# Attention's main loop ordered by timed events, the product with v in two lumps a pair

## The chip, the cores and the metric

One core of a Trainium2 chip runs the whole program. The metric is the device time of one execution in microseconds, the median of the runs of one kernel. Five engines matter here: TensorE (PE in the rows, its weight loads PEld), VectorE (DVE), ScalarE (ACT), GpSimd (POOL), and SyncE (SP), which here only issues DMAs. Each works through its own queue in order.

## The reference

What is computed is attention with rotary positions over 4 batches of 8 heads (576 positions, 64 wide), and two feed-forward layers on its output.

```python
def _attn_ref(q, k, v):                 # 4, 8, 576, 64
    ...
    q_rot, k_rot = (rotate(q), rotate(k))
    scores = scale * np.matmul(q_rot, k_rot.transpose(0, 1, 3, 2))
    scores = scores - np.max(scores, axis=-1, keepdims=True)
    attn = np.exp(scores)
    attn = attn / (np.sum(attn, axis=-1, keepdims=True) + 1e-09)
    return np.matmul(attn, v).astype(np.float32)

def reference(**kwargs):
    ...
    x = np.ascontiguousarray(attn_out.transpose(0, 2, 1, 3)).reshape(B * S, H * D)
    x = _moe_ref(x=x, **moe_kwargs)     # (max(x @ w_in, 0) ** 2) @ w_out, 2304 x 512, 2048 wide
    return _moe2_ref(x=x, **moe2_kwargs)  # leaky relu with alpha between two products
```

## The kernel before

Attention runs first, the two feed-forward layers (`moe`) after it. The change touches attention alone.

Attention works on 16 pairs of heads, one after another. The two heads of a pair (index j) lie side by side in the tiles. A pair has nine steps, (i, j) for four blocks i of 128 queries and both heads, and one step (4, 0) for the last 64 queries of both heads together.

In each step `scores` multiplies a block of q with all keys: k is split into a high and a low part (kH, kL), so a block is four matmuls, and ten in step (4, 0). They fill one of two score buffers `sc` (two PSUM banks each). VectorE takes the row maximum (L201), ScalarE the exp (L202), which writes the probabilities to `p` and their sum to `sums`. The next block for that buffer waits for the exp. Four steps later (LAG) `trans` turns the probabilities with four transpositions (L223) into a bank of the pool `ps_t`, and `leave` copies the bank to `pt`, on ScalarE and VectorE by turns. `trans_tail` (L235, L241, L242) does that for the 64 columns that are left over. `over` adds 1e-9 to the sums, takes their reciprocal (VectorE), transposes them (L254), and ScalarE copies and stores them to `rd`. `pv` multiplies the turned probabilities with v (L273), in two halves of 288 queries (hf 0 and 1), ten matmuls each; one matmul appears in the trace as two records. A half is copied to `st`, by VectorE for hf 0 (L278), by ScalarE for hf 1 (L280), and then stored to `xd` (L281).

The next pair's q and k come from `rope` on GpSimd. `turn` transposes them (L145, L151), each into a bank of `ps_t`; ScalarE copies the bank to the high part of `nat` (L139) and VectorE subtracts it from the bank for the low part (L140). `stack` then copies `nat` to kH, qT and kL with 12 DMAs of 144 KB on SP (L166). There is one `nat`.

PSUM has eight banks: four for the two score buffers, three for `ps_t` (NTB), one for the product with v (`ps_a`, NAC).

The order on TensorE and SP is the order in which the Python code issues (a manual schedule). ScalarE and VectorE follow a planner that goes by its own costs and that also chooses which free bank a tile gets. The loop goes over steps s: it issues the scores of step s, the transpositions of step s - 4, and then whatever `at_step` has put at s. The turning of the next pair stands at the pair's steps 0, 1 and 2 (the last with the tail and the stack). The sums follow straight after the tail of step (4, 0). The product with v stands in six lumps (LUMPS), of 4, 4 and 2 matmuls for each half, one behind each of the six steps after it; in the last pair each half is one lump. During the last 24 steps `follow` starts the loads and the first weight conversions of `moe`.

Of the kernel before, what the change touches and what calls it, by code (L numbers as in the profile page):

```python
# [22 lines left out]
P = 128  # L23
# [5 lines left out]
NQ = 5  # L29
NR = 10  # L30
SCALE = D ** -0.5

LAG = 4
# [6 lines left out]
OP0, OPD0, OP1, OPD1 = 1, 1, 0, 1  # L40
OP, OPD = 1, 1


def attention(tc, q, k, v, ident_d, rope_d, xd, rd, follow):
# [10 lines left out]
    with ExitStack() as at:  # L55
# [17 lines left out]
        ps_t = pool("ps_t", NTB, space=PSUM)  # L73
        ps_a = pool("ps_a", NAC, space=PSUM)

# [8 lines left out]

        pairs = [(b, hp) for b in range(B) for hp in range(NPAIR)]
        rot = {}
# [44 lines left out]

        def turn(n):


            nt = nat.tile([P, 2, 2, S + 64], F32R, name="nat")
            r4 = {nm: rot[n, nm].rearrange("p r j d -> p r (j d)") for nm in "kq"}

            def split(pv, view):
                A.activation(out=view(0), in_=pv, func=AF.Copy)  # L139
                V.tensor_tensor(out=view(1), in0=pv, in1=view(0).bitcast(F32), op=ALU.subtract)  # L140

            def main(x, nm):
                u = ps_t.tile([P, 512], F32, name="ps", tag="t")
                for c in range(4):
                    T.transpose(u[:, c * P:(c + 1) * P], r4[nm][:, c], ident)  # L145
                split(u, lambda y: nt[:, y, x, 64:576])

            def tail():
                u = ps_t.tile([P, 512], F32, name="ps", tag="t")
                for x, nm in enumerate("kq"):  # L150
                    T.transpose(u[:, x * P:(x + 1) * P], r4[nm][:, 4], ident)  # L151
                split(u[:, 0:256].rearrange("p (x z c) -> p x z c", x=2, z=2),
                      lambda y: nt[:, y].rearrange("p x (z c) -> p x z c", c=64)[:, :, 0:10:9])

            def stack():
                qT = qTs[n % 2]
                kH = kq.tile([P, 2 * S], F32R, name="kH")
                kL = kq.tile([P, 2 * S], F32R, name="kL")
                ops[n] = qT, kH, kL
                f = nt.bitcast(F32)  # L160
                for j in range(2):
                    for o, y, x, gap in ((kH, (0, 0), 0, 0), (qT, (0, 1), 1, 64), (kL, (1, 1), 0, 0)):
                        c0, o0 = 64 * (1 - j), j * (S + gap)
                        for z in range(2):
                            E = nc.scalar if z and n == 0 else nc.sync
                            E.dma_start(out=o[64 * z:64 * z + 64, o0:o0 + S].bitcast(F32),  # L166
                                        in_=f[64 * j:64 * j + 64, y[z], x, c0:c0 + S])

            def last():
                tail()  # L170
                stack()

            return [(main, 0, "k"), (main, 1, "q"), (last,)]

# [29 lines left out]

        turns = itertools.cycle((A, V))

        def leave(dst, src):
            E = next(turns)
            if E is A:
                A.activation(out=dst, in_=src, func=AF.Copy)  # L210
            else:
                V.tensor_copy(out=dst, in_=src)  # L212

        def trans(n, i, j):

            if (i, j) == (0, 0):
                PT[n, "tail"] = pt.tile([P, S], F32, name="ptt")
            if i == 0:
                PT[n, j] = pt.tile([P, 4, S], F32, name=f"pt{j}")
            p = Pt[n, i]  # L220
            u = ps_t.tile([P, 512], F32, name="ps", tag="t")
            for c in range(4):
                T.transpose(u[:, c * P:(c + 1) * P], p[:, (S + 64) * j + c * P:(S + 64) * j + (c + 1) * P], ident)  # L223
            uv = u.rearrange("p (c x) -> p c x", c=4)
            if i < 4:
                leave(PT[n, j][:, :, i * P:(i + 1) * P], uv)
            else:
                for x in range(2):
                    leave(PT[n, x][:, :, 512:576], uv[:, :, 64 * x:64 * x + 64])

        def trans_tail(n, i0, i1):

            u = ps_t.tile([P, 512], F32, name="ps", tag="t")
            for i in range(i0, min(i1, 4)):
                T.transpose(u[:, (i - i0) * P:(i - i0 + 1) * P], Pt[n, i][:, 512:640], ident)  # L235
            m = min(i1, 4) - i0
            if m:
                leave(PT[n, "tail"][:, i0 * P:(i0 + m) * P], u[:, 0:m * P])
            if i1 == 5:

                T.transpose(u[0:64, m * P:(m + 1) * P], Pt[n, 4][:, 512:576], ident)  # L241
                T.transpose(u[:, (m + 1) * P:(m + 2) * P], Pt[n, 4][:, 448:576], ident)  # L242
                for x in range(2):
                    rs, u0 = slice(64 * x, 64 * x + 64), (m + x) * P + 64 * x
                    leave(PT[n, "tail"][rs, 512:576], u[rs, u0:u0 + 64])

# [13 lines left out]

        accs = {}

        def pv(n, hf, c0, c1):
            b, hp = pairs[n]
            v2 = raw[n // 2 % 2, "v"][:, 2 * (n % 2):2 * (n % 2) + 2]
            sl = slice(hf * SH, (hf + 1) * SH)
            if c0 == 0:
                accs[hf] = ps_t.tile([P, 512], F32, name="ps", tag="t") if (n, hf) == (len(pairs) - 1, 1) else ps_a.tile([P, 512], F32, name="acc")
            acc = accs[hf]
# [14 lines left out]
        order = [(i, j) for i in range(4) for j in range(2)] + [(4, 0)]  # L284
        steps = [(n, i, j) for n in range(len(pairs)) for i, j in order]
        per = len(order)
        load(0, "k", 0, 1, nc.gpsimd)
# [11 lines left out]
        rope(0, "q", 5, NR, V)  # L299
        for f, *a in turn(0):  # L300
            f(*a)
        load(0, "v")
        for nm in "kqv":
            load(1, nm)
        later = {}

        def at_step(s, f, *a):
            later.setdefault(s, []).append((f, a))

        rope(1, "k")  # L310
        rope(1, "q", E=V)

        for s in range(len(steps) + LAG + OP + len(LUMPS) * OPD + 8):
            if s < len(steps):
                n, i, j = steps[s]
                at = s % per
                if at == 0 and n + 1 < len(pairs):
                    for x, (f, *a) in zip(TURN_AT, turn(n + 1)):
                        at_step(s + x + (1 if n == 0 else 0), f, *a)
                if at == ROPE_AT and n + 2 < len(pairs):  # L320

                    for m in range(n + 2, n + 4 if n + 4 == len(pairs) else n + 3):
                        for nm in "kq":
                            if (m, nm) not in rot:
                                rope(m, nm)
                    if n % 2 and n + 3 < len(pairs):
                        for nm in "kq":
                            load((n + 3) // 2, nm)
                        at_step(s - ROPE_AT + V_AT, load, (n + 3) // 2, "v")
                scores(n, i, j)  # L330
            if LAG <= s and s - LAG < len(steps):
                n, i, j = steps[s - LAG]
                last = n + 1 == len(pairs)
                trans(n, i, j)
                if (i, j) == ((2, 1) if last else (3, 1)):
                    trans_tail(n, 0, 3 if last else 4)
                    if last:
                        at_step(s + OP0, pv, n, 0, 0, 5)
                if (i, j) == (4, 0):
                    trans_tail(n, 3 if last else 4, 5)  # L340
                    at_step(s, over, n)
                    for x, lump in enumerate(LUMPS):
                        if not last:
                            at_step(s + OP + x * OPD, pv, n, *lump)
                    if last:
                        at_step(s + OP1, pv, n, 1, 0, 5)
            for f, a in later.pop(s, []):
                f(*a)
            if s == len(steps) - AHEAD_X:
                front.close()  # L350
            if s == len(steps) - 1:
                scored.close()
            if s >= len(steps) - AHEAD_X:
                follow()

# [388 lines left out]
```

## Time and profile before

| | us |
|---|---|
| median of 3 runs | 1159.99 |
| lowest and highest run | 1159.45 to 1165.15 |
| the profiled execution | 1164.05 |
| its span, first to last instruction | 1162.3 |

The page gives, for each engine, its busy time and share of the span; the longest part of the span is the feed-forward layers, which are TensorE work almost without a gap. Attention ends at 351.86 us of the span, where the first matmul of `moe` starts. Records of TensorE overlap (a matmul is still draining when the next starts), so its busy time hides short waits; distances between starts don't.

### The profile page before, as it was taken

To read this page: it belongs to the slowest core of one execution; us is meant where nothing else is said; L and a number is where in the kernel's file an instruction comes from. 1 tells how busy PE (TensorE), PEld (TensorE's weight loads), DVE (VectorE), ACT (ScalarE), POOL (GpSimd) and SP (SyncE) were. 2 spreads that over 40 slices of the span, in tenths; PEclk is the share of its full clock that TensorE was granted. 3 is DMA by queue.
4 is the path that set the end of the run, shared out by engine and by line. 5 is a ranking of instruction groups with operands and counts; after the bars stand their busy time and mean duration, and the time that the engine had idled before them with its cause. 6 is when DMAs were issued, how large, how long until landed. Compare 5 with 4: busy or idle time off the path is not lost.

```text
span 1162.3 us, 17534 instructions
## 1 busy us (share of the span) xinstructions
PE 1108.2 (95%) x6480; PEld 987.0 (85%) x6480; DVE 615.5 (53%) x1094; ACT 526.2 (45%) x1116; POOL 311.3 (27%) x304
## 2 busy tenths in 40 slices
PE   2899999999988999999999999999999999999997
PEld 1676666666658999999999999998998989898996
DVE  3666666666567897858677670323232332323231
ACT  1656565656555874455555644223232222323221
POOL 3663366236340000012120201032230404132140
PEclk9999999999999999999999999999999999999999
DMA  7757556654753442455657447830101001010101
GB/s 184 177 138 179 144 127 169 171 149 123 190 168 108 146 133 88 165 167 201 222 188 256 159 166 253 270 109 14 41 7 48 1 28 27 19 36 14 28 1 27
DMA packets 91733, 140.73 MB, mean 121 GB/s; under 512 B 21120, under 2 KB 62720, under 8 KB 91648
## 3 DMA queue, kind: packets, MB, share of 16 engines
q1 hardware_dynamic: 87856, 133.24, 39.3%
q10 hardware_dynamic: 3536, 6.24, 1.6%
q8 instruction: 51, 0.84, 0.3%
q14 instruction: 34, 0.28, 0.1%
q0 software_dynamic: 256, 0.13, 0.0%
HBM read 80.26 MB, written 31.01 MB: 96 GB/s over the span
## 4 chain that ended last, share of the span: by engine, by line
PE 83%; DVE 6%; SPq 4%; DMA 3%; issue 1%; ACT 1%; ACTq 0%; DVEq 0%
PE py L564 31%; PE ph L546 11%; PE ph L548 11%; PE ph L547 11%; PE acc L273 6%; PE sc L198 6%; PE ps L223 3%; PE ph L564 2%; DVE nm L201 2%; SPq L166 2%; DVE nat L140 1%; DMA qraw<-in_q_dram 1%; DVE pt L212 1%; SPq L107 1%; SPq L103 1%
## 5 line engine op out<-in xcount | busy, mean ns | idle before, releaser
L546 PE MATMUL ph<-xs,w 128*128 128x384 f32 x768 | 257.5, 335 | 3.5 <-ACT g L586 3.5
L547 PE MATMUL ph<-xs,w 128*128 128x384 f32 x768 | 257.3, 335 | 0.0
L548 PE MATMUL ph<-xs,w 128*128 128x384 f32 x768 | 257.2, 335 | 0.0
L501 DVE TENSOR_TENSOR gl<-g,gh 128x384 fp32r<-128x384 f32 x192 | 110.4, 576 | 174.7 <-PE py L564 124.2
L586 ACT ACTIVATE g<-ph 128x384 f32<-128x384 f32 x192 | 94.3, 491 | 207.9 <-PE ph L548 198.5
L590 POOL TENSOR_TENSOR g<-g,xt 128x384 f32<-128x384 f32 x96 | 101.8, 1061 | 295.6 <-DVE xt L589 295.6
L494 ACT ACTIVATE gh<-g 128x384 fp32r<-128x384 f32 x192 | 100.6, 524 | 163.0 <-PE py L564 147.6
L201 DVE TENSOR_REDUCE nm<-sc 128x1 f32<-128x576 f32 x144 | 108.7, 755 | 104.8 <-PE sc L198 103.7
L564 PE MATMUL py<-w,gh 128*128 128x512 f32 x504 | 155.2, 389 | 0.0
L546 PEld LDWEIGHTS ph<-xs,w 128*128 128x128 f32 x768 | 144.6, 188 | 4.4 <-ACT g L586 3.8
L564 PE MATMUL py<-gh,w 128*128 128x384 f32 x560 | 146.5, 336 | 0.0
L547 PEld LDWEIGHTS ph<-xs,w 128*128 128x128 f32 x768 | 144.6, 188 | 0.2
L548 PEld LDWEIGHTS ph<-xs,w 128*128 128x128 f32 x768 | 144.7, 188 | 0.0
L202 ACT ACTIVATE p<-sc,nm 128x576 f32<-128x576 f32 x144 | 106.5, 739 | 83.6 <-DVE nm L201 72.7
L589 DVE TENSOR_SCALAR xt<-ph,al 128x384 f32<-128x384 f32 x96 | 59.3, 618 | 138.8 <-ACT g L586 133.1
L564 PEld LDWEIGHTS py<-w,gh 128*128 128x128 f32 x504 | 94.5, 188 | 19.4
L564 PEld LDWEIGHTS py<-gh,w 128*128 128x128 f32 x560 | 102.0, 189 | 0.0
L564 PE MATMUL py<-w,gl 128*128 128x512 f32 x252 | 98.1, 389 | 0.0
L564 PE MATMUL py<-gl,w 128*128 128x384 f32 x280 | 94.2, 336 | 1.8 <-DVE gl L501 1.8
L198 PE MATMUL sc<-kH,qT 128*128 128x288 f32 x336 | 83.7, 335 | 10.0 <-DMA qT<-nat 7.6
L223 PE MATMUL ps<-ident,p 128*128 128x128 f32 x576 | 88.0, 276 | 2.6 <-ACT pt L210 0.7
L198 PEld LDWEIGHTS sc<-kH,qT 128*128 128x128 f32 x336 | 51.4, 193 | 45.1 <-issue 29.2
(107 smaller groups left out, 1588.2 us busy)
## 6 DMA issues: line engine op xcount, KB each, us to landing
w<-in_moe_w_in_dram SPq DMA_DIRECT2D x32, 512.0 KB
w<-in_moe_w_out_dram SPq DMA_DIRECT2D x32, 512.0 KB
wk<-xs SPq DMA_DIRECT2D x32, 512.0 KB
w<-wk SPq DMA_DIRECT2D x30, 512.0 KB
xt<-x SPq DMA_DIRECT2D x48, 192.0 KB
kH<-nat SPq DMA_DIRECT2D x62, 144.0 KB
qT<-nat SPq DMA_DIRECT2D x62, 144.0 KB
kL<-nat SPq DMA_DIRECT2D x62, 144.0 KB
```

Source lines behind the costliest of these rows:

```text
L198: T.matmul(sc[:, hf, o0:o0 + w], lhsT=lhs, rhs=kx[:, c0:c0 + w], start=st and y == 0, stop=not st and y == len(prods) - 1 and o0 + w == SH)
L201: V.tensor_reduce(out=nm, in_=sc[:, :, 0:SH], axis=AX.XY, op=ALU.max, negate=True)
L202: A.activation(out=Pt[n, i][:, j * S:(j + 1) * S].rearrange("p (a b) -> p a b", a=2), in_=sc[:, :, 0:SH], func=AF.Exp, bias=nm, accum_out= ...
L223: T.transpose(u[:, c * P:(c + 1) * P], p[:, (S + 64) * j + c * P:(S + 64) * j + (c + 1) * P], ident)
L494: A.activation(out=hi, in_=hidden(layer, b, i), func=AF.Copy)
L501: V.tensor_tensor(out=lo, in0=hidden(layer, b, i), in1=gsp[u][0].bitcast(F32), op=ALU.subtract)
L546: T.matmul(ph[:, :W], lhsT=wh[:, cs], rhs=xh, start=(c == 0), stop=False)
L547: T.matmul(ph[:, :W], lhsT=wh[:, cs], rhs=xl, start=False, stop=False)
L548: T.matmul(ph[:, :W], lhsT=wl[:, cs], rhs=xh, start=False, stop=(c == KC - 1))
L564: T.matmul(acc, lhsT=x, rhs=y, start=(s0 and k == 0), stop=(s1 and k == 2))
L586: A.activation(out=g, in_=ph, func=AF.Relu)
L590: G.tensor_tensor(out=g, in0=g, in1=mn, op=ALU.add)
```

## The change

The steps of the loop become events with a time, in steps, and are issued in the order of these times; equal times keep the order in which they were registered. For a pair that starts at step s:

- scores stay at s + 0 to s + 8; transpositions stand at s + 4 + T_AT;
- the turning of the next pair's k, q and tail, and the stack, at s + 0.9, 2.1, 3.2 and 3.6 (in the first pair 1.3, 2.3, 3.3, 3.3);
- the two tails at s + 10.7 and 12.0, the sums at s + 13.01;
- each half of the product with v is one lump of ten matmuls, at s + 13.3 and s + 15.3; the last pair has its own times;
- there is no bank for accumulators alone: `ps_t` has four banks, and a half of the product takes one of them;
- which engine copies a turned block out is given by the string SIDES, and no longer alternates;
- the load of v for a later couple of pairs stands at s + 21.1, ahead of a stack, where it stood behind it.

No product, transposition, copy or transfer is added or left out.

```diff
-NP_, NSC, NTB, NAC = 6, 2, 3, 1
+NP_, NSC, NTB, NAC = 6, 2, 4, 0
-ROPE_AT, TURN_AT, V_AT = 5, (0, 1, 2), 21
-LUMPS = ((0, 0, 2), (0, 2, 4), (0, 4, 5), (1, 0, 2), (1, 2, 4), (1, 4, 5))
+ROPE_AT, V_AT = 5, 21
+TURN0, TURN_AT = (1.3, 2.3, 3.3, 3.3), (0.9, 2.1, 3.2, 3.6)
+T_AT = (0.6, 0.6, 0.1, 1.1, 0.6, 0.6, 0.6, 0.6, 0.6)
+TAIL_AT, OVER_AT = (6.7, 8.0), 9.01
+PV_AT = (9.3, 11.3)
+PV_LAST = (6.35, 8.4)
+SIDES = 'AVAAAVAVAVAVAV'
...
-        def leave(dst, src):
-            E = next(turns)
-            if E is A:
+        def leave(dst, src, side):
+            if side == "A":
                 A.activation(out=dst, in_=src, func=AF.Copy)
             else:
                 V.tensor_copy(out=dst, in_=src)
...
-        def pv(n, hf, c0, c1):
+        def pv(n, hf):
...
+            acc = ps_t.tile([P, 512], F32, name="ps", tag="t") if NAC == 0 or (n, hf) == (len(pairs) - 1, 1) else ps_a.tile([P, 512], F32, name="acc")
-            for c in range(c0, c1):
+            for c in range(NQ):
                 for j in range(2):
                     t = PT[n, j][:, c, sl] if c < 4 else PT[n, "tail"][:, sl]
                     T.matmul(acc[64 * j:64 * j + 64, 0:SH], lhsT=v2[:, j, c], rhs=t, start=c == 0, stop=c == 4)
-            if c1 < NQ:
-                return
...
+        def at(t, f, *a):
+            events.append((t, len(events), f, a))
...
+        for n in range(pairs_n):
+            s, last = n * per, n + 1 == pairs_n
+            for x, (i, j) in enumerate(order):
+                at(s + x, scores, n, i, j)
+                at(s + x + LAG + (.1 if last else T_AT[x]), trans, n, i, j)
+            if not last:
+                for x, (f, *a) in zip(TURN_AT if n else TURN0, ((turn, "k"), (turn, "q"), (turn_tail,), (stack,))):
+                    at(s + x, f, n + 1, *a)
+            if n + 2 < pairs_n:
+                at(s + ROPE_AT - .1, ropes, n)
+            if last:
+                at(s + 5 + LAG + .2, trans_tail, n, 0, 3)
+                at(s + 8 + LAG + .2, trans_tail, n, 3, 5)
+                at(s + LAG + 8.3, over, n)
+                for hf, t in enumerate(PV_LAST):
+                    at(s + LAG + t, pv, n, hf)
+            else:
+                at(s + LAG + TAIL_AT[0], trans_tail, n, 0, 4)
+                at(s + LAG + TAIL_AT[1], trans_tail, n, 4, 5)
+                at(s + LAG + OVER_AT, over, n)
+                for hf, t in enumerate(PV_AT):
+                    at(s + LAG + t, pv, n, hf)
...
+        while events:
+            events.sort(key=lambda e: e[:2])
+            _, _, f, a = events.pop(0)
+            f(*a)
```

## Rows read from the trace of the kernel before

**Rows 1.** The page, part 1: busy us (share of the span) and instructions of each engine.

```profile
PE 1108.2 (95%) x6480; PEld 987.0 (85%) x6480; DVE 615.5 (53%) x1094; ACT 526.2 (45%) x1116; POOL 311.3 (27%) x304
```

**Rows 2.** Busy us by stretch: length, PE, PEld, DVE, ACT, POOL, granted clock, DMA, GB/s.

```profile
201.36:221.20 19.84, 18.95 (x138) 13.59 (x136) 12.70 (x22) 11.78 (x31) 3.00 (x3) 1.00 0.56 144
209.50:218.20 8.70, 8.66 (x61) 5.65 (x61) 4.93 (x9) 5.06 (x14) 0.00 (x0) 1.00 0.90 207
343.00:351.86 8.86, 6.08 (x34) 3.24 (x32) 5.12 (x12) 1.60 (x5) 0.00 (x0) 0.81 0.26 84
```

**Rows 3.** TensorE's timeline with lumps: start us, us, line, operation, [idle before].

```profile
213.03 1.19 PE L273 MATMUL acc<-pt,vraw 128*64 128x288 f32 x8
214.16 0.53 PE L198 MATMUL sc<-kH,qT 128*128 128x288 f32 x2
...
215.31 0.71 PE L273 MATMUL acc<-ptt,vraw 128*64 128x288 f32 x4
215.95 0.53 PE L198 MATMUL sc<-kH,qT 128*128 128x288 f32 x2
```

**Rows 4.** TensorE's timeline, steps without a lump, and the next pair's L254.

```profile
203.57 0.51 PE L198 MATMUL sc<-kH,qT 128*128 128x288 f32 x2
...
204.19 0.60 PE L223 MATMUL ps<-ident,p 128*128 128x128 f32 x4
204.62 0.60 PE L145 MATMUL ps<-ident,rotq 128*128 128x128 f32 x4
204.98 0.51 PE L198 MATMUL sc<-kH,qT 128*128 128x288 f32 x2
...
205.89 0.63 PE L223 MATMUL ps<-ident,p 128*128 128x128 f32 x4
206.55 0.66 PE L235 MATMUL ps<-ident,p 128*128 128x128 f32 x4
207.30 0.33 PE L151 MATMUL ps<-ident,rotk 128*128 128x128 f32 x1
...
208.65 0.27 PE L242 MATMUL ps<-ident,p 128*128 128x128 f32 x1
209.54 0.27 PE L254 MATMUL ps<-ident,sums 128*32 128x128 f32 x1 [0.62 <-DVE nat L140]
...
229.28 0.27 PE L254 MATMUL ps<-ident,sums 128*32 128x128 f32 x1 [0.62 <-DVE nat L140]
```

**Rows 5.** TensorE's timeline at the end of attention.

```profile
340.48 2.16 PE L273 MATMUL acc<-pt,vraw 128*64 128x288 f32 x16
...
346.24 0.30 PE L241 MATMUL ps<-ident,p 128*64 128x128 f32 x1 [1.99 <-ACT ptt L210]
...
347.66 3.79 PE L273 MATMUL ps<-pt,vraw 128*64 128x288 f32 x16
```

**Rows 6.** VectorE's timeline in the lump-free steps.

```profile
204.38 0.76 DVE L201 TENSOR_REDUCE nm<-sc 128x1 f32<-128x576 f32 x1 [0.84 <-PE sc L198]
205.06 0.68 DVE L140 TENSOR_TENSOR nat<-ps,nat 128x512 fp32r<-128x512 f32 x1
...
208.98 0.41 DVE L140 TENSOR_TENSOR nat<-ps,nat 128x256 fp32r<-128x256 f32 x1
```

**Rows 7.** ScalarE's timeline there.

```profile
205.18 0.74 ACT L202 ACTIVATE p<-sc,nm 128x576 f32<-128x576 f32 x1 [0.57 <-DVE nm L201]
...
205.91 0.59 ACT L210 ACTIVATE pt<-ps 128x512 f32<-128x512 f32 x1
206.39 0.60 ACT L139 ACTIVATE nat<-ps 128x512 fp32r<-128x512 f32 x1
```

**Rows 8.** TensorE's timeline in the first pair.

```profile
35.49 0.53 PE L198 MATMUL sc<-kH,qT 128*128 128x288 f32 x2 [0.44 <-ACT p L202]
...
38.13 0.53 PE L198 MATMUL sc<-kH,qT 128*128 128x288 f32 x2 [0.44 <-ACT p L202]
```

**Rows 9.** SP's timeline: the first DMAs of a stack.

```profile
208.53 1.10 SPq L166 DMA_DIRECT2D kH<-nat  x2
```

More of the change, by code (lines that the diff above doesn't have):

```diff
@@ L73, in attention @@
         ps_t = pool("ps_t", NTB, space=PSUM)
-        ps_a = pool("ps_a", NAC, space=PSUM)
+        ps_a = pool("ps_a", NAC, space=PSUM) if NAC else None
         tab = cp.tile([P, NR, 3, HALF], F32, name="tab")
@@ L83, in table @@
             A.activation(out=tabq[:, 5 * j:5 * j + 5], in_=tab[:, 5 * j:5 * j + 5], func=AF.Copy, scale=SCALE)
-        pairs = [(b, hp) for b in range(B) for hp in range(NPAIR)]
+        pairs = [(b, hp) for b in range(B) for hp in range(NPAIR)][:PAIRS]
         rot = {}
@@ L130, in attention @@
             G.memset(t[:, S:S + 64].bitcast(F32), 0.0)
[L132 to L173, printed above, removed]
@@ new lines, in attention, with split, turn @@
+        nats = {}
+        def split(dst, src, sl):
+            hi, lo = dst
+            A.activation(out=sl(hi), in_=src, func=AF.Copy)
+            V.tensor_tensor(out=sl(lo), in0=src, in1=sl(hi).bitcast(F32), op=ALU.subtract)
+        def turn(n, nm):
+            if nm == "k":
+                nats[n] = nat.tile([P, 2, 2, S + 64], F32R, name="nat")
+            r4 = rot[n, nm].rearrange("p r j d -> p r (j d)")
+            u = ps_t.tile([P, 512], F32, name="ps", tag="t")
+            for c in range(4):
+                T.transpose(u[:, c * P:(c + 1) * P], r4[:, c], ident)
+            split([nats[n][:, y, nm == "q"] for y in range(2)], u, lambda t: t[:, 64:576])
@@ L225, in trans @@
             if i < 4:
[L226 removed]
+                leave(PT[n, j][:, :, i * P:(i + 1) * P], uv, SIDES[2 * i + j])
             else:
                 for x in range(2):
[L229 removed]
+                    leave(PT[n, x][:, :, 512:576], uv[:, :, 64 * x:64 * x + 64], SIDES[8 + x])
         def trans_tail(n, i0, i1):
@@ L237, in trans_tail @@
             if m:
-                leave(PT[n, "tail"][:, i0 * P:(i0 + m) * P], u[:, 0:m * P])
+                leave(PT[n, "tail"][:, i0 * P:(i0 + m) * P], u[:, 0:m * P], SIDES[10])
             if i1 == 5:
@@ L244, in trans_tail @@
                     rs, u0 = slice(64 * x, 64 * x + 64), (m + x) * P + 64 * x
-                    leave(PT[n, "tail"][rs, 512:576], u[rs, u0:u0 + 64])
+                    leave(PT[n, "tail"][rs, 512:576], u[rs, u0:u0 + 64], SIDES[12 + x])
         def over(n):
@@ L284, in attention, with ropes @@
         order = [(i, j) for i in range(4) for j in range(2)] + [(4, 0)]
-        steps = [(n, i, j) for n in range(len(pairs)) for i, j in order]
-        per = len(order)
+        per, pairs_n = len(order), len(pairs)
+        events = []
+        def at(t, f, *a):
+            events.append((t, len(events), f, a))
+        def ropes(n):
+            for m in range(n + 2, n + 4 if n + 4 == pairs_n else n + 3):
+                for nm in "kq":
+                    if (m, nm) not in rot:
+                        rope(m, nm)
+            if n % 2 and n + 3 < pairs_n:
+                for nm in "kq":
+                    load((n + 3) // 2, nm)
+                at(9 * n + V_AT + .1, load, (n + 3) // 2, "v")
         load(0, "k", 0, 1, nc.gpsimd)
@@ L299, in attention @@
         rope(0, "q", 5, NR, V)
-        for f, *a in turn(0):
-            f(*a)
+        turn(0, "k")
+        turn(0, "q")
+        turn_tail(0)
+        stack(0)
         load(0, "v")
@@ L304, in attention @@
             load(1, nm)
-        later = {}
-        def at_step(s, f, *a):
-            later.setdefault(s, []).append((f, a))
         rope(1, "k")
         rope(1, "q", E=V)
[L313 to L354, printed above, removed]
@@ L357 @@
+        end = pairs_n * per
+        at(end - AHEAD_X + .9, front.close)
+        at(end - 1 + .9, scored.close)
+        for s in range(end - AHEAD_X, end + LAG + 14):
+            at(s + .95, follow)
+        while events:
+            events.sort(key=lambda e: e[:2])
+            _, _, f, a = events.pop(0)
+            f(*a)
 NB, W = 6, 384
```

27 lines of the change are left out of this document (20 added, 7 removed).

## Prediction

> **What bounds the kernel now.** I read the page's busy line first [rows 1]: TensorE is busy 95% of the span, no other engine over 53%. That is an average, so the next view is the busy time by stretch. One pair of heads in the middle of attention [rows 2] takes 19.84 us with TensorE busy in 18.95, VectorE 12.70, ScalarE 11.78: TensorE sets the pace, but its records overlap, and a busy share cannot tell work from lost time. So I read TensorE's timeline and took distances from start to start. The sums' transposition comes at 209.54 and again at 229.28 [rows 4], one pair = 19.74 us (the 13 periods from the second pair on lie between 19.74 and 19.86). Inside, two kinds of time are lost.
>
> First, the product with v. A score block of four matmuls plus four transpositions costs 203.57 to 204.98, less the 0.43 of the k/q turning in it (204.19 to 204.62): 0.97 us [rows 4]. With a lump of 4 records of L273 the step takes 214.16 to 215.95 = 1.79; from lump to next score, 8 records take 1.13 and 4 take 0.64 [rows 3], so four more cost 0.49. The 4-record lump should cost 0.49 and costs 1.79 - 0.97 = 0.82: **a toll of 0.33 us for each lump**, whatever its length. A full 20-record lump exists once, in the last pair: 16 records end 2.16 us after 340.48 [rows 5], no dearer per record. A lump-of-all should thus cost 5 x 0.49 + 0.33 = 2.8.
>
> Second, waits for PSUM banks, in the steps without a lump [rows 4]: score to transposition 0.91 (204.98 to 205.89) where 0.62 is normal (203.57 to 204.19); then 0.66 to L235 and 0.75 to L151 where 0.43 is normal; then 0.89 from L242 to L254 where a transposition takes 0.11. Together 0.29 + 0.23 + 0.32 + 0.78 = 1.62; the same four distances in twelve pairs between 60 and 300 us have medians that make 1.55. VectorE shows the cause [rows 6]: the subtraction of the turned k ends at 205.74, just before 205.89; that of the tail ends at 209.39, and the wait that 209.54 shows is put down to it. A turned block holds its bank until ScalarE has copied it and VectorE has subtracted, behind reductions.
>
> **The change part by part.**
> *Two lumps in place of six.* Four tolls fewer in each of 15 pairs (the last pair has two lumps already): 15 x 4 x 0.33 = **19.8 us**, all of it on TensorE, which sets the end. Matmul and transposition counts stay.
>
> *Accumulators among four transposition banks.* Transpositions get a fourth bank whenever no lump is open. A lump now needs one of the four, and returns it after the copy to st. Between the lumps stand only three groups of transpositions and two score blocks, so the second lump finds a bank. The first starts soon after the last turned block and may wait for its subtraction.
>
> *Turning and sums moved.* k is turned after step 0.9, q after 2.1, the tail after 3.2, the reciprocal sums come behind step 4's scores, not straight behind the tails. That takes away the 0.78 wait, and spreads the turned blocks between other transpositions. If all of today's waits go: 14 x 1.55 = **21.7 us** (pairs with a turning and a pair before them).
>
> *What is late next.* The new order leaves seven score blocks (7, 8, 0 to 4) without a lump between the second lump and the next first one. In that stretch TensorE has 7 blocks at 0.97 - 0.43 = 0.54, six extra products of the ten-product block (0.135 each), and 41 transpositions at 0.109: 3.8 + 0.8 + 4.5 = 9.0 us. ScalarE has, start to start [rows 7], seven exps at 0.73 (205.18 to 205.91), six 512-wide copies at 0.48 (SIDES gives it transpositions 3, 4, 6 and the tail; two are turned blocks), and some 1.2 of small ones: 9.2. VectorE: seven reductions at 0.68, start to start (204.38 to 205.06), four 512-wide operations at 0.68 each [rows 6], 1.3 small ones: 8.8. The three engines are level there, where today TensorE leads in every step with a lump. The rest of a pair (two lumps, two score blocks, twelve transpositions) is 5.6 + 1.1 + 1.3 = 8.0, so TensorE alone would make a pair in 17.0 us, against 19.74.
>
> The unknown is how much TensorE waits per pair in that stretch; call it s. From below: the score ring. There are two score buffers, and a block waits until the exp of the block two earlier has read its buffer. At the start of attention, where nothing else holds TensorE, a block comes 35.49 to 38.13 = 2.64 us after the one two before, waiting 0.44 for the exp [rows 8]. Block 4 follows block 7 by three such links, 7.9 us, and TensorE's own work up to it is 9.0 - 0.5 = 8.5: no wait, s = 0. From above: each link gets one ScalarE copy and one VectorE operation more than those rows had, 2.64 + 0.48 + 0.68 = 3.80; three links are 11.4, s = 2.9. I take **s = 0.7**, half of today's waits, nearer the lower end: the links of rows 8 already hold one leaving copy each, and 9.2 us of ScalarE in seven steps is 2.63 per link, as much as the link and not more.
>
> *SIDES.* ScalarE takes five of eight main blocks and always the big tail, today they alternate: about 1 us a pair moves from VectorE to ScalarE. Both sums above hold it.
>
> *The 12 stacking DMAs and the v load on SP.* The stack is issued after step 3.6 rather than in step 2. The steps before it lose their lump, so that is still about 7 us after the pair's first block (now 201.36 to 208.53) [rows 2, 9]. Its transfers start a microsecond later and fill the DMA engines for 8.7 us (share 0.90, 207 GB/s) [rows 2]: they are bound by bandwidth. They would end some 17 us after the first block; block 1 of the next pair needs the last of them at 17.6 + 1.4 = 19. That is a cover of 2 us at most, where today it is 4 (218.2 against 221.2 + 1.4). The v load (after 21.1) now stands ahead of a stack on SP; its buffer is free long before, so SP issues it right behind the previous stack, in an idle stretch. The next k and q loads come forward by it. Cost nothing; if the cover goes, at most 1 us per pair at block 1, which s up to 2.9 includes. POOL's rotations keep their order. The st copy and its store on ScalarE's queue meet the end of the stack: some tenths of the cover.
>
> *First pair, last pair, MoE.* The first turning keeps its place; the last pair's lumps too. What follows attention is issued relative to its steps and moves with its end: nothing.
>
> **The sum.** 19.8 + 14 x (1.55 - 0.7) = 19.8 + 11.9 = 31.7 us. The profiled execution took 1164.05 (span 1162.3) and would become 1132; the median of the three runs is 1159.99, 4 us lower, and I subtract from that: **1128 us**.
>
> **A rule weighed.** The whole pair, lump-free steps included, shows a granted clock of 1.00, TensorE's 2.4 GHz level [rows 2]. In 343 to 351.9 its mean is 0.81: after TensorE had stood for 1.99 us, 16 records took 3.79 where 2.16 is normal [rows 2, 5]. The Trainium skill, "TensorE: Matmul & The Clock Gate", Part 4: PE-mode transpose, says transpositions do not count as busy for the clock gate the way matmuls do; by that rule the 9-us stretch, now without v products, could lose the clock. The trace's lump-free steps, which kept it, speak against that.
>
> **The rivals.**
> (a) *The ring and the banks eat the second part.* s between 1.5 and 2.9. For it: three engines level, single in-order queues, two score buffers; and a block that turns holds its bank for two operations. Against: rows 8. 1160.0 - 41.5 + 14 s: 1139 to 1159.
> (b) *The score ring makes it slower.* Same place, but each link carries two waits on VectorE (a reduction behind a subtraction) besides the copy: 2.64 + 0.48 + 2 x 0.68 = 4.48, three links 13.4, s = 4.9: 1160 - 41.5 + 69 = 1187. It decides from s = 3.0 (41.5 / 14). For it: SP and TensorE follow a written order, so a late exp stops the transpositions behind it as well. Against: VectorE's queue puts a reduction ahead of a subtraction that would not be ready (step 1's at 204.38, the turned k's of step 0 at 205.06) [rows 6].
> (c) *The toll does not go with the lump count.* If what I call a toll belongs to the v products themselves, only the waits are won: 1160 - 11.9 = 1148. Against: the 4- and 8-record lumps agree on it.
> (d) *The clock falls in the lump-free stretch.* Work there grows by 3.79 / 2.16 = 1.75: 14 x 9.0 x 0.75 = 94 us, 1223.
>
> **How the numbers follow.** Forecast (s from 0 to 1.5: 1118 to 1139) 0.62; (a) 0.19; (c) 0.07; (b) with milder forms from s = 2.9 on 0.10; (d) 0.02. The range 1117 to 1151 takes the forecast, (c) and the lower half of (a), about 0.8. A measurement of this kernel can tell about 0.5%, 6 us: faster by more than that 0.86 (forecast, (c), nearly all of (a)), within it 0.05 (ends of (a) and (b)), slower 0.09.
>
> **What would show it.** The distance between two sums' transpositions: 17.6 us if right, 17.0 to 18.5 within the forecast, over 19.7 for (b). Two groups of L273 a pair, 2.8 us from the transposition before to the next block. The waits of L254 for the tail's subtraction gone. New waits, where there are any, on scores for the exp (ring), on the first lump for the turned q or tail (bank), on scores for the stack DMA (cover gone). The prediction falls if waits of scores for the exp exceed 1.5 us per pair, or if L273 loses no more time than now yet the period stays.

## The result, and the profile after

The changed kernel takes 1132.65 us (median; 1132.03 to 1133.43). The ratio of its runs to those of the kernel before on the same chip is 0.975 (95% interval 0.972 to 0.979), some 29 us less (27.3 between the two medians). Its profiled execution took 1133.05 us with a span of 1131.3; before it was 1164.05 and 1162.3. The page's busy line of the changed kernel, the answer to [rows 1]:

```profile
PE 1088.7 (96%) x6480; PEld 996.4 (88%) x6480; DVE 600.3 (53%) x1070; ACT 535.6 (47%) x1140; POOL 312.3 (28%) x304
```

TensorE has as many instructions as before in 19.5 us less busy time. Waits are no busy time, so part of the gain lies inside the records, where a toll for switching would lie.

Line numbers moved: scores L198 is now L196, the reduction L199, the exp L200, the copies of turned blocks L205 and L207, transpositions L218, the tails L230, L236 and L237, the sums L246 (addition), L247 (reciprocal) and L249 (transposition), the turning L149 and L155, the product with v L264, the stack's DMAs L170, the subtraction of the turned k and q L141. Some of the kernels below have these lines one further down. TensorE's timeline of one pair after (start us, us, engine, line, operation), against [rows 3, 4]:

```profile
169.86 0.27 PE L249 MATMUL ps<-ident,sums 128*32 128x128 f32 x1
170.06 2.16 PE L264 MATMUL ps<-pt,vraw 128*64 128x288 f32 x16
172.05 0.66 PE L264 MATMUL ps<-ptt,vraw 128*64 128x288 f32 x4
172.64 0.66 PE L218 MATMUL ps<-ident,p 128*128 128x128 f32 x4
...
174.63 0.60 PE L218 MATMUL ps<-ident,p 128*128 128x128 f32 x4
175.16 2.16 PE L264 MATMUL ps<-pt,vraw 128*64 128x288 f32 x16
177.15 0.66 PE L264 MATMUL ps<-ptt,vraw 128*64 128x288 f32 x4
177.73 0.52 PE L196 MATMUL sc<-kH,qT 128*128 128x288 f32 x2
...
185.05 0.30 PE L236 MATMUL ps<-ident,p 128*64 128x128 f32 x1 [0.23 <-DVE nat L141]
...
187.64 0.27 PE L249 MATMUL ps<-ident,sums 128*32 128x128 f32 x1
```

A half of the product is one lump; from its start to the next instruction go 2.58 and 2.57 us for 20 records. From the transpositions ahead of it to the next instruction go 2.78 and 3.10 us; less these transpositions (0.11 and 0.43) a lump costs 2.67, where the prediction had 2.8. L249 has no wait left. From 177.73 to 187.64 there is no lump. The busy time by stretch of the changed kernel (columns as in [rows 2]), for this pair, for the lump-free stretch ahead of it, for ScalarE's and VectorE's work on that stretch's seven blocks (from the first exp to the last, from the first reduction to the last), for most of attention, and for two places that come up below:

```profile
169.86:187.64 17.78, 17.50 (x137) 13.87 (x135) 12.08 (x21) 12.49 (x31) 17.23 (x16) 1.00 0.63 153
160.60:169.80 9.20, 9.20 (x76) 8.86 (x75) 6.89 (x13) 7.85 (x20) 0.77 (x1) 1.00 0.99 228
162.32:172.49 10.17, 10.17 (x84) 8.61 (x83) 7.96 (x15) 9.27 (x24) 3.38 (x4) 1.00 0.91 208
161.53:171.63 10.10, 10.10 (x85) 9.03 (x85) 8.71 (x16) 8.44 (x22) 2.60 (x3) 1.00 0.91 208
50.00:250.00 200.00, 199.61 (x1572) 160.75 (x1571) 131.68 (x230) 142.89 (x357) 110.77 (x95) 1.00 0.74 180
289.50:293.30 3.80, 3.80 (x19) 3.77 (x20) 1.45 (x2) 1.81 (x4) 1.64 (x3) 0.55 0.76 199
314.00:320.00 6.00, 5.49 (x22) 2.48 (x23) 1.74 (x5) 0.34 (x2) 0.00 (x0) 0.50 0.28 88
```

TensorE works 199.6 of 200 us at a granted clock of 1.00. In the lump-free stretch ahead of this pair it is busy without a gap (9.20 us), ScalarE 7.85 and VectorE 6.89. These two come later to the same seven blocks and are busy for 9.27 and 8.71 us until they are through with them, close to the 9.2 and 8.8 of the prediction; what doesn't fit into the stretch they do beside the next lump. A period is the distance from one transposition of the sums to the next. The thirteen that begin with the second pair are 17.02 or 17.03 us in eight cases, and 17.46, 17.19, 17.79, 17.57 and 17.53 in five; together 223.8, where the kernel before has 257.0 (308.35 - 51.34). That is 33.2 us. The next period is the first that is longer than before, 21.39 against 17.45, and here SP and TensorE read so (their timelines after; SPq is SP's DMA queue):

```profile
256.50 1.15 SPq L170 DMA_DIRECT2D kH<-nat  x2
...
275.97 0.33 SPq L500 DMA_DIRECT2D xt<-x  x1
276.35 1.08 SPq L502 DMA_DIRECT2D xt<-r  x2
277.47 1.23 SPq L170 DMA_DIRECT2D kH<-nat  x2
```

```profile
256.80 0.27 PE L249 MATMUL ps<-ident,sums 128*32 128x128 f32 x1
273.83 0.27 PE L249 MATMUL ps<-ident,sums 128*32 128x128 f32 x1
...
287.91 0.50 PE L196 MATMUL sc<-kH,qT 128*128 128x288 f32 x2 [2.21 <-DMA qT<-nat]
289.38 0.52 PE L196 MATMUL sc<-kL,qT 128*128 128x288 f32 x2 [0.98 <-DMA kL<-nat]
289.73 1.03 PE L218 MATMUL ps<-ident,p 128*128 128x128 f32 x4
```

In the middle pairs the stack starts 0.30 us before L249 (256.50, 256.80). The last pair's starts 3.64 behind it (277.47), because loads of `x` and `r` for the first feed-forward layer (L500, L502) stand ahead of it on SP. Scores of the last pair then wait 2.21 and 0.98 us, and four transpositions take 1.03 where 0.60 is usual: the granted clock of that stretch is 0.55.

The balance of the two profiled executions: the first pair +1.3 us, thirteen periods +33.2, the boundary to the last pair -3.9, the last pair +2.4 (19.29 against 21.65), from its sums to the first matmul of the feed-forward layers -0.9 (319.81 - 314.51 against 351.86 - 347.45), those layers -1.1 (811.5 against 810.4); sum 31.0 with rounding (1164.05 - 1133.05).

### The profile page after: what moved, and what is told of

It reads as the page before. It is cut to its first block, busy times and chain, and to the rows that moved or that the text cites. A ratio compares the mean times of both kernels' runs of the same rounds, so it can differ in the third digit from the quotient of the medians.

```text
span 1131.3 us, 17531 instructions
## 1 busy us (share of the span) xinstructions
PE 1088.7 (96%) x6480; PEld 996.4 (88%) x6480; DVE 600.3 (53%) x1070; ACT 535.6 (47%) x1140; POOL 312.3 (28%) x304
## 4 chain that ended last, share of the span: by engine, by line
PE 87%; DMA 4%; DVE 3%; SPq 3%; ACT 1%; issue 1%; POOL 0%; ACTq 0%; DVEq 0%; POOLq 0%
PE py L553 32%; PE ph L535 12%; PE ph L536 12%; PE ph L537 12%; PE ps L264 7%; PE sc L196 6%; PE ps L218 4%; PE ph L553 2%; DMA vraw<-in_v_dram 2%; SPq L170 2%; PE ps L149 1%; DMA xt<-r 1%; DVE nm L199 1%; DMA kL<-nat 1%; PE ps L230 1%
## 5 line engine op out<-in xcount | busy, mean ns | idle before, releaser
L483 ACT ACTIVATE gh<-g 128x384 fp32r<-128x384 f32 x192 | 100.5, 524 | 160.6 <-PE py L553 145.2
L199 DVE TENSOR_REDUCE nm<-sc 128x1 f32<-128x576 f32 x144 | 108.0, 750 | 84.2 <-PE sc L196 83.6
L200 ACT ACTIVATE p<-sc,nm 128x576 f32<-128x576 f32 x144 | 107.0, 743 | 45.3 <-DVE nm L199 36.2
L196 PE MATMUL sc<-kH,qT 128*128 128x288 f32 x336 | 82.2, 331 | 12.6 <-DMA qT<-nat 11.3
L218 PE MATMUL ps<-ident,p 128*128 128x128 f32 x576 | 87.1, 279 | 0.2
L510 POOL TENSOR_TENSOR xt<-xt 128x384 f32<-128x384 f32 x24 | 27.5, 1149 | 216.6 <-DMA xt<-x 172.5
```

Source lines behind the costliest of these rows:

```text
L196: T.matmul(sc[:, hf, o0:o0 + w], lhsT=lhs, rhs=kx[:, c0:c0 + w], start=st and y == 0, stop=not st and y == len(prods) - 1 and o0 + w == SH)
L199: V.tensor_reduce(out=nm, in_=sc[:, :, 0:SH], axis=AX.XY, op=ALU.max, negate=True)
L200: A.activation(out=Pt[n, i][:, j * S:(j + 1) * S].rearrange("p (a b) -> p a b", a=2), in_=sc[:, :, 0:SH], func=AF.Exp, bias=nm, accum_out= ...
L483: A.activation(out=hi, in_=hidden(layer, b, i), func=AF.Copy)
```

## The experiments

Each kernel differs from the changed one by the edit shown, unless it says otherwise. The whole time varies by some us between chips and includes ends that the edits don't aim at, so the third column has what most of them are about: the thirteen periods in the profiled execution. The fourth has the two periods behind them.

| kernel | ratio to before (95%) | 13 periods, us | the last two |
|---|---|---|---|
| before | 1 | 257.0 | 39.1 |
| changed | 0.975 (0.972 to 0.979) | 223.8 | 40.7 |
| changed, on another chip | 0.970 (0.968 to 0.972) | 223.6 | 38.7 |
| before with two lumps | 0.986 (0.983 to 0.989) | 238.4 | 40.8 |
| bank of its own | 0.977 (0.973 to 0.980) | 229.0 | 41.0 |
| bank of its own, six lumps | 1.003 (1.001 to 1.004) | 260.5 | 37.8 |
| sums early | 0.972 (0.969 to 0.975) | 223.6 | 42.3 |
| turning at the old steps | 0.975 (0.972 to 0.978) | 227.6 | 41.3 |
| tail and stack late | 0.979 (0.976 to 0.982) | 230.6 | 40.5 |
| all copies on ScalarE | 0.984 (0.982 to 0.986) | 240.7 | 38.6 |
| one lump | 0.978 (0.976 to 0.980) | 234.6 | 38.4 |
| last stack first | 0.971 (0.970 to 0.973) | 223.4 | 39.4 |
| last stack and turning first | 0.970 (0.967 to 0.972) | 224.6 | 40.4 |
| no addition | 0.970 (0.967 to 0.973) | 221.4 | 40.6 |

**Before with two lumps.** The kernel before, with one lump for each half, two steps apart.

```diff
-LUMPS = ((0, 0, 2), (0, 2, 4), (0, 4, 5), (1, 0, 2), (1, 2, 4), (1, 4, 5))
+LUMPS = ((0, 0, 5), (1, 0, 5))
-OP, OPD = 1, 1
+OP, OPD = 1, 2
```

> The kernel before with one edit: two lumps of ten matmuls a pair in place of six, in its own order, with three transposition banks and an accumulator bank. Theory (a toll of 0.33 us for each lump of the product with v, four fewer in 15 pairs): the period of a pair falls from 19.76 to about 18.4 us, 19.8 us in all, about 1140; the waits for banks stay, L254's 0.6 us per pair among them. Rival (c), the toll belongs to the v products and not to the lump: the period stays, 1160. Rival, the freed time turns into longer waits of the lump-free steps: between the two.

It took 1144.0 us, 17.4 less than before on that chip; the thirteen periods lost 18.7, 1.44 a pair. The waits of TensorE between 48 and 275 us in this kernel (us in total, times, longest):

```profile
PE ps L254 <- DVE nat L140: 3.9, 7, 0.6
PE ps L151 <- DVE pt L212: 3.8, 6, 0.7
```

The waits for banks stay, in other places. So the toll goes with the number of lumps; each of the four is worth 0.29 us by the whole time and 0.36 by the periods, and these numbers still hold what the waits changed. The next two kernels part the two.

**A bank of its own for the product, and with it six lumps.** The first takes the fourth transposition bank back, the second also the two lumps; what stays in it are the moved times and SIDES. The code by which `pv` does a part of a half again is left out of the second edit.

```diff
-NP_, NSC, NTB, NAC = 6, 2, 4, 0
+NP_, NSC, NTB, NAC = 6, 2, 3, 1
```

```diff
-PV_AT = (9.3, 11.3)
+PV_AT = (9.3, 10.3, 11.3, 12.3, 13.3, 14.3)
+LUMPS = ((0, 0, 2), (0, 2, 4), (0, 4, 5), (1, 0, 2), (1, 2, 4), (1, 4, 5))
```

> The kernel after with one edit: three transposition banks and one bank for accumulators alone, as before; two lumps, the times of the events and SIDES stay. If the fourth transposition bank is what took the waits away, the lump-free steps wait again, 0.8 to 1.5 us per pair: 11 to 21 us, 1144 to 1154. If the spreading of the turned blocks and of the sums took them away, at most 3 us are lost: 1133 to 1136.

> The kernel after with three transposition banks and one accumulator bank, and with the product with v in the six lumps of before, one a step at the pair's steps 4.3 to 9.3 of the next pair. Against the run with an own bank it differs by the lumps alone: by the toll it is 15 x 4 x 0.33 = 19.8 us slower than that one. If the lumps' number costs nothing by itself, both take the same time; since lumps in every step give ScalarE and VectorE time to catch up, it could even be faster.

The waits of TensorE in the same stretch, with the bank of its own, and then with six lumps besides:

```profile
PE ps L218 <- DVE nat L141: 2.1, 11, 0.5
```

```profile
PE ps L219 <- DVE nat L142: 11.1, 12, 1.0
```

With three banks the common period is 17.53 to 17.54 us instead of 17.02, so the fourth bank is worth 0.4 us a pair in the mean (5.2 in thirteen), and TensorE waits for the subtraction of a turned block as it did before. With six lumps the period is 20.04, more than the 19.77 before: the moved times alone gain nothing. From six lumps to two, with the same banks, are 2.43 us a pair. Where they lie is read by cutting the period at the first transposition of the turned k (`rotk`): all lumps stand ahead of it, none behind it. TensorE's timeline with the bank of its own, and then with six lumps besides:

```profile
192.38 0.27 PE L249 MATMUL ps<-ident,sums 128*32 128x128 f32 x1
...
203.93 0.60 PE L149 MATMUL ps<-ident,rotk 128*128 128x128 f32 x4
...
209.90 0.27 PE L249 MATMUL ps<-ident,sums 128*32 128x128 f32 x1
```

```profile
190.06 0.28 PE L250 MATMUL ps<-ident,sums 128*32 128x128 f32 x1
...
202.86 0.60 PE L150 MATMUL ps<-ident,rotk 128*128 128x128 f32 x4
...
210.09 0.27 PE L250 MATMUL ps<-ident,sums 128*32 128x128 f32 x1
```

The first part takes 11.55 or 11.56 us with two lumps and 12.80 or 12.81 with six, in all thirteen periods, with equally many records and no wait listed: 1.25 us for four tolls, 0.31 each. The rest is 5.97 here against 7.23: longer waits for that subtraction (listed are 0.16 and 0.99; shorter ones hide in the records). The same cut gives a first part of 13.40 to 13.47 before and 12.18 to 12.21 with two lumps alone, again 0.31 a toll, and a rest that varies between 5.55 and 7.04 in the latter. So a lump costs the same in both orders, and the waits make the difference: two lumps bring 18.7 us in the old order and 31.5 in the new one. What TensorE does in the 0.31 us is not shown.

**Sums early.** The sums go ahead of the last score block again.

```diff
-TAIL_AT, OVER_AT = (6.7, 8.0), 9.01
+TAIL_AT, OVER_AT = (6.7, 8.0), 8.65
```

> The kernel after with one edit: the sums' transposition straight behind the last block of step (4, 0) (event 12.65 in place of 13.01), ahead of the next score block. Theory that the place of the sums was worth 0.78 us a pair: it waits for a bank again, 14 x 0.6 to 0.8 = 8 to 11 us, 1141 to 1144. Rival: with four banks there is a free one by then, at most 2 us, 1132 to 1135.

No wait for the sums' bank comes back; the periods are 16.93 to 17.81, the thirteen 223.6, as in the changed kernel. With four banks and two lumps, where the sums stand makes no difference.

**Turning at the old steps; tail and stack late.** First the times of the turning nearest to those before; then k and q as changed, the tail one step and the stack 0.65 of a step later.

```diff
-TURN0, TURN_AT = (1.3, 2.3, 3.3, 3.3), (0.9, 2.1, 3.2, 3.6)
+TURN0, TURN_AT = (1.3, 2.3, 3.3, 3.3), (0.9, 1.9, 2.65, 2.7)
```

```diff
-TURN0, TURN_AT = (1.3, 2.3, 3.3, 3.3), (0.9, 2.1, 3.2, 3.6)
+TURN0, TURN_AT = (1.3, 2.3, 3.3, 3.3), (0.9, 2.1, 4.2, 4.25)
```

> The kernel after with one edit: q turned at 1.9 (ahead of block 2's scores, as before), the tail and the stack at 2.65 and 2.7 (behind the transpositions of step 2, as before). Theory that the spreading of the turned blocks took the banks' waits away: they come back, 0.5 to 1.2 us a pair, 7 to 17 us, 1140 to 1150. Rival, the fourth bank and the two lumps did: the periods stay within 0.2 us. And as the stack then starts a step earlier, the last pair's wait for it (3.2 us and the half clock behind it) goes as well: 1128 to 1132.

> The kernel after with one edit: the tail's turning at 4.2 and the stack at 4.25, a step later, straight ahead of the first lump. By the prediction the stack's cover is 2 us at most; a step is some 1.3 us and the copies behind it take some tenths more. If the cover is about 1 us, block 1 of the next pair waits for the stack, 0.5 to 1.5 us a pair: 7 to 21 us, 1140 to 1154, with waits of L196 for kL. If the cover is 2 us or more: within 2 us of the kernel after.

The waits of TensorE between 48 and 275 us, turning at the old steps, and then tail and stack late:

```profile
PE ps L236 <- ACT ptt L205: 1.2, 4, 0.3
PE ps L155 <- DVE nat L141: 0.8, 2, 0.4
```

```profile
PE sc L196 <- ACT p L200: 2.2, 6, 0.5
PE sc L196 <- DMA kL<-nat: 2.2, 4, 1.1
PE sc L196 <- DMA qT<-nat: 0.4, 1, 0.4
```

Spreading the turning is worth 0.3 us a pair (227.6 against 223.8). In the second kernel the stack starts 0.93 us behind the sums' transposition (172.92, 171.99) where the changed kernel has it 0.30 ahead, 1.2 us later. In three pairs scores then wait 0.2 to 0.7 us for its transfers; in a fourth, the last of the thirteen, up to 1.1, but there a load of `x` already stands ahead of the stack, which starts 2.4 behind the sums. In the changed kernel no score in this stretch waits for a transfer. The cover that the change leaves is thus 0.5 to 1 us in the three pairs, and at least the 1.2 us of the delay in the others. The old steps don't shorten the boundary to the last pair (21.75): the loads on SP still stand ahead of its stack, at 279.8 to 281.3.

**All copies on ScalarE; one lump.** The first moves five of the copies from VectorE to ScalarE, the second puts both halves of the product together, so that the rest of the pair is one stretch of nine blocks.

```diff
-SIDES = 'AVAAAVAVAVAVAV'
+SIDES = 'AAAAAAAAAAAAAA'
```

```diff
-PV_AT = (9.3, 11.3)
+PV_AT = (9.3, 9.31)
```

> The kernel after with one edit: ScalarE copies all turned blocks out (three more 512-wide copies, a half and a small one: some 2 us a pair move from VectorE to it). If the three engines are level in the lump-free stretch, as the prediction's sums of 9.0, 9.2 and 8.8 us say, TensorE now waits for ScalarE, 1 to 2 us a pair: 15 to 30 us, 1148 to 1163. If ScalarE has slack there, at most 3 us: 1133 to 1136.

> The kernel after with one edit: both halves of the product with v one behind the other, 20 matmuls in one lump, at the place of the first. The toll theory alone: one toll of 0.33 us less in 15 pairs, 5 us faster, 1128. Against it, the theory of level engines: all nine score blocks now stand without a lump between them, TensorE has 11.9 us there, and ScalarE and VectorE more than that with the two blocks' copies, so that TensorE waits for them, 0.5 to 1.5 us a pair: 1135 to 1150. The two halves also hold two banks at once.

The waits in the same stretch, all copies on ScalarE, and then one lump:

```profile
PE ps L218 <- ACT pt L205: 11.9, 12, 1.0
```

```profile
PE sc L196 <- ACT p L200: 10.1, 26, 0.5
```

The common periods are 18.33 and 17.99 us. With all copies on ScalarE that engine sets the pace: transpositions wait 1 us a pair for its copies. With one lump scores wait twice a pair for the exp, 0.31 and 0.47 us, but ScalarE isn't full there. It stands idle for the reduction ahead of the first of these exps, and starts the second (183.76) as its reduction ends (183.73):

```profile
182.50 0.74 ACT L200 ACTIVATE p<-sc,nm 128x576 f32<-128x576 f32 x1 [0.44 <-DVE nm L199]
```

So it is the ring of two score buffers, which rival (a) feared, with its chain of score, reduction and exp: it binds where four blocks stand straight behind the long lump, and nowhere in the changed kernel. From start to start the two blocks take 1.52 and 1.27 us (181.86, 183.38, 184.65) where 0.96 and 0.54 are usual, 1.29 more; without that the pair would take 16.70, 0.32 less than 17.02, as one toll fewer should.

**The last stack first.** The steps of the feed-forward layer's start that fell ahead of the last pair's stack are put behind it; in the second kernel the last turning stands at the old steps as well. Beside that one the changed kernel ran again.

```diff
-            at(s + .95, follow)
+            at(max(s + .95, end - 14.3) if end - 18 <= s < end - 14 else s + .95, follow)
```

```diff
-                for x, (f, *a) in zip(TURN_AT if n else TURN0, ...
+                for x, (f, *a) in zip((TURN_AT if n < pairs_n - 2 else (0.9, 1.9, 2.65, 2.7)) if n else TURN0, ...
-            at(s + .95, follow)
+            at(max(s + .95, end - 15.25) if end - 18 <= s < end - 15 else s + .95, follow)
```

> The kernel after with one edit: the calls of follow that stand ahead of the last pair's stack on SP (its steps 0.95 to 3.95 of the pair before) come straight behind it. In the kernel after, the last pair's first blocks wait 2.2 and 1.0 us for the stack, with half the clock for some 4 us behind that. Theory (the loads of x, held up by their buffers, hold up the stack on SP): the stack starts some 4 us earlier, these waits go, and the distance between the two last sums but one falls from 21.4 to about 16 us: 4 to 5.5 us faster, 1127 to 1129. Rival: bandwidth, not the order on SP, makes the stack late: same time within 1 us. Rival: the delayed loads of x hold up the first layer: the gain is given back there.

> The kernel after with two edits near its end: the last turning stands earlier (q at 1.9, tail and stack at 2.65 and 2.7), and the calls of follow from step 126 on come straight behind that stack on SP. With the calls moved alone, a wait of 1.2 us for kL was left. Theory (SP's order makes the last stack late): that wait shrinks to under 0.5 us, 1127.5 to 1129. Rival: the wait that is left is bandwidth shared with the loads of x, and stays: 1129 to 1130.

> The kernel after, unchanged, beside the run above on the same chip: 1131 to 1134. It sets the length of the last pairs against that run's.

The boundary shrinks to 17.86 and 17.20 us, so the loads on SP were its cause. But the next period grows to 21.59 and 23.24. In the second kernel VectorE's and TensorE's timelines show why:

```profile
298.67 1.13 DVE L384 TENSOR_SCALAR m<-w 128x512 uint32<-128x512 uint32 x1 [5.88 <-DMA w<-in_moe_w_in_dram]
...
300.09 0.74 DVE L199 TENSOR_REDUCE nm<-sc 128x1 f32<-128x576 f32 x1
```

```profile
301.75 0.53 PE L196 MATMUL sc<-kH,qT 128*128 128x288 f32 x2 [2.15 <-ACT p L200]
```

The weights' load, now later, keeps VectorE idle ahead of L384 for 5.88 us, and behind that instruction stand the reduction (300.09) that the exp needs, and TensorE waits for the exp. Behind that wait of 2.15 us the granted clock is 0.60 for 3.8 us (301.70 to 305.50). What the stack wins, the last pair gives back. On the same chip the changed kernel has 1128.8 us and this one 1128.0: no better. The changed kernel's own two profiles differ at this place too (21.39 and 19.18 us for the boundary), so the gain of the first of these two kernels (0.971 against 0.975, on different chips) isn't shown.

## Why the prediction was right

It said 1128 us (1117 to 1151) and a gain of 31.7; measured are 1132.65, a gain of 27.3 between the medians, 29 by the ratio and 31.0 between the profiled executions. Step by step:

- **The toll**: right. 0.33 us a lump was read from single steps; 0.31 is what each of four costs in the part of the pair that holds the lumps, in the old order and in the new one. Rival (c), which gave the whole change only the waits, falls with that kernel.
- **TensorE alone, 17.0 us a pair**: right, the common period is 17.02.
- **s = 0.7, the new wait per pair**: mis-sized. The mean period is 17.21, so s is 0.2, and that comes from VectorE's addition beside GpSimd (last section), which the prediction didn't have: without it the mean is 17.03 and the ring costs nothing. The links of rows 8, with one copy each, were the right guide, and the allowance on top of them was not needed. In thirteen periods the gain is 33.2, of which 13 x 1.25 = 16.3 are toll; toll and waits were to bring 13 x (1.32 + 0.85) = 17.2 + 11.0 = 28.2.
- **"That takes away the 0.78 wait"**, the place of the sums: wrong cause. With the sums early again nothing is lost. With two lumps alone the wait of L254 stays, 0.56 us on average in seven pairs; with three banks in the new order waits for the same subtraction turn up at L218. The two lumps, the moved times and the fourth bank took the bank waits away together.
- **"First pair, last pair, MoE: nothing"**: wrong. I had followed the stack past the steps, but not the loads for the next stage that stand ahead of it on SP in the last turning. In the kernel before, the same loads stand there and make the stack 2.7 us late (310.04, the sums at 308.35; in a middle pair 208.53 and 209.54 [rows 4, 9]), which its cover hid: that boundary is 17.45. Now it is 3.9 us late and the cover is thinner, and the boundary takes 3.9 us more than before. Outside the thirteen periods 31.7 - 28.2 = 3.5 us were forecast, and -2.2 came.
- So the total came out this well by luck: two errors, +5.0 and -5.7 us, cancelled. On the other chip the boundary takes 19.18 us, 1.7 more than before, and the gain is 35 us (1163.9 to 1128.8), more than forecast.
- **The stack's cover, cost nothing**: right in the middle pairs, where no score waits for a transfer; 1.2 us later it fails in some pairs.
- **Rivals (a) and (b)**, ring and banks: no score waits for an exp in the thirteen periods. The places that they named are the right ones, but the changed kernel stays clear of them: one lump fewer brings waits for the exp in every pair, a later tail some, and five copies more on ScalarE bring waits for the copies.
- **Rival (d)**, the clock: the lump-free stretch kept the 2.4 GHz level (1.00 in 160.6 to 169.8). The rule of the Trainium skill weighed in the prediction ("TensorE: Matmul & The Clock Gate", Part 4: PE-mode transpose) did not come to bear in this stretch, where score products stand between the transpositions.

## What to carry to other kernels

Measure what a switch between two kinds of matmul costs from distances of starts, step with and step without, and lump what can be lumped; but test the order and the lumps together, since the new order with six lumps (and three banks) was slower here than the old one. The moved load of v and the new times of the transpositions were not tested alone. When a step is moved later, look at the pair at each end of the loop for what another stage has put ahead of it on the same queue: what a wide cover had hidden came out once it was thin. And when the biggest engine has no slack left, look for small instructions of unusual length on the others.

## What was not expected of the hardware

Five of the thirteen periods are 0.2 to 0.8 us longer than 17.02. VectorE, GpSimd and ScalarE in one of them (the changed kernel's timeline), behind VectorE's addition of the pair before, where GpSimd stands still:

```profile
165.43 0.16 DVE L246 TENSOR_SCALAR sums<-sums 128x9 f32<-128x9 f32 x1
...
182.14 1.57 POOL L128 TENSOR_TENSOR rotk<-t,t 128x640 f32<-128x640 f32 x1
182.44 1.30 DVE L246 TENSOR_SCALAR sums<-sums 128x9 f32<-128x9 f32 x1
...
183.65 0.74 DVE L199 TENSOR_REDUCE nm<-sc 128x1 f32<-128x576 f32 x1
...
184.32 0.67 DVE L141 TENSOR_TENSOR nat<-ps,nat 128x512 fp32r<-128x512 f32 x1
184.43 0.74 ACT L200 ACTIVATE p<-sc,nm 128x576 f32<-128x576 f32 x1 [0.66 <-DVE nm L199]
184.92 0.20 DVE L247 RECIPROCAL sums<-sums 128x9 f32<-128x9 f32 x1
185.04 0.69 DVE L199 TENSOR_REDUCE nm<-sc 128x1 f32<-128x576 f32 x1
```

The addition of 1e-9 to nine columns takes 0.16 us in one pair and 1.30 in the next, where it ends with GpSimd's instruction (182.44 + 1.30 = 183.74, 182.14 + 1.57 = 183.71). Behind it the reduction, the exp (0.66 idle) and the subtraction come late, and TensorE waits 0.23 us at 185.05 for a bank. The reductions, the subtraction and the reciprocal keep their length beside GpSimd. In the kernel before the same addition takes 0.15 to 0.87 us (0.33 on average), yet the periods vary by only 0.12: there its delay is hardly passed on. The test leaves the addition out:

```diff
-            V.tensor_scalar(t, t, 1e-9, None, ALU.add)
```

> The changed kernel without the addition of 1e-9 to the sums (left out: that addition). In the changed kernel VectorE's addition (128x9) takes 0.16 to 0.17 us when GpSimd is idle, and 0.69 to 1.30 us where one of GpSimd's instructions for the turning runs beside it; it then ends together with that instruction. The reciprocal behind it takes 0.20 to 0.22 us in all 16 pairs. Theory: the addition waits for GpSimd's instruction, and that is what makes the pairs with 17.2 to 17.8 us between the transpositions of the sums longer than the others, which have 17.02. Without it all thirteen periods lie within 16.95 to 17.1, sum 221.3 us instead of 223.8; the time falls by about 2.5 us, a ratio 0.002 lower than that of the changed kernel, or by less if the last pair or the MoE stage gives it back. Rival: the longer periods come from the transfers that these pairs have more of, or from GpSimd's instructions slowing all of VectorE; then every second period stays at 17.2 to 17.8 and the time is that of the changed kernel. Second rival: the reciprocal, now first, takes the addition's place beside GpSimd and shows 0.7 to 1.3 us; then the periods stay as well, and the row of the reciprocal says so.

The reciprocal of that kernel, all its instructions grouped (shortest, median and longest in ns, first and last start):

```profile
L246 DVE RECIPROCAL sums<-sums x16: 204/204/216, 40.2 to 309.8; 128x9 f32<-128x9 f32 x16
```

The reciprocal, now alone, has not taken the addition's place. All thirteen periods are 17.02 to 17.04 us, together 221.4 instead of 223.8, with the same transfers and the same work on GpSimd: the addition was the cause of the long ones. The whole time is 1127.7 us (ratio 0.970), less than the first measurement of the changed kernel and the same as its second (0.970), so the 2.4 us are shown in the periods and not in the whole time.

The Trainium skill, "SBUF — State Buffer", section "Who interferes with whom", says that VectorE in a two-port mode, which `tensor_scalar` can enter, shares a pair of ports with GpSimd, that the pair is locked for a whole instruction, and that the other side blocks; `tensor_reduce` never contends on trn2. The rows agree with both: 1.30 us for the addition, and 0.74 for the reduction beside GpSimd's next instruction. In which mode the addition ran, no row shows.

Of the clock: after TensorE's waits of 2.21 and 0.98 us ahead of the last pair, the granted clock was 0.55, near the 1.2 GHz level, for 3.8 us. In the second profile of the changed kernel, after waits of 1.61 and 1.06 us at the same place, it did not fall (1.00 from 287.21 to 291.50; TensorE's timeline there):

```profile
285.65 0.50 PE L196 MATMUL sc<-kH,qT 128*128 128x288 f32 x2 [1.61 <-DMA qT<-nat]
287.21 0.51 PE L196 MATMUL sc<-kL,qT 128*128 128x288 f32 x2 [1.06 <-DMA kL<-nat]
287.56 0.60 PE L218 MATMUL ps<-ident,p 128*128 128x128 f32 x4
```

This place differs by 2.2 us between the two profiles of one kernel: 0.5 us are waits, and 1.6 lie between the second wait and the sums' transposition (289.38 to 295.23 against 287.21 to 291.50), where four transpositions take 0.60 us instead of 1.03. At the end of attention the granted clock is 0.50 after (314 to 320 us), and 16 records take 4.11 us (314.81) where before took 3.79 [rows 5]: that cost stayed.
